# One gather per block of the second layer instead of three at once, and the next expert's first weight splits two blocks later

## The chip, the core and the metric

The program runs on one core of one Trainium2 chip. The metric is the time of one execution on the device in microseconds (us). The core's engines are called by their short names: PE multiplies matrices (PEld is its loading of weights), DVE works element by element, ACT evaluates functions, POOL is the general engine that here makes some element-wise work and issues all indirect DMAs, SP issues the plain DMAs. Each engine executes its own instructions strictly in program order and waits on semaphores for the others.

## The reference, cut to what matters

A gated linear attention over 4 x 768 tokens gives rows of 384 numbers. Each of the 3072 rows is then assigned to one of 8 experts (384 rows each, taken by the size of the router's logits), goes through that expert's two-layer network, and then through a second network that is the same for all rows:

```python
for e in range(E):                       # E = 8
    mask = assigned == e                 # 384 rows
    h = np.maximum(x[mask] @ w1[e], 0.0) # 384 -> 1024
    out[mask] = h @ w2[e]                # 1024 -> 384
...
h = x @ w_in                             # 384 -> 2048
sp = np.where(h > 20.0, h, np.log1p(np.exp(np.minimum(h, 20.0))))
g = h * np.tanh(sp)
return (g @ w_out).astype(np.float32)    # 2048 -> 384
```

All of it is float32. A product of float32 numbers is made of three matrix products: each operand is split into a rounded high part and a low remainder (`...h` and `...l` in the names), and high x high, low x high and high x low are added up.

## The kernel before, in words

The first 183 us are the attention and the routing of the first expert. Then a loop over the experts k = 0 to 7 runs (`for k in range(E)` in `tile_moe`), each with two phases on 384 gathered rows:

- the **first layer**, 8 blocks f of 128 hidden units: `h1` multiplies, `h1_parts` splits the result, `y1` multiplies by the second weight. The weight splits `split_w1(k, f)` (high part `w1h` on ACT, L914; low part `w1l` on POOL, L915) are made two blocks ahead, in two buffers each. Those of blocks 0 and 1 of the next expert are made during the second layer of this one.
- the **second layer**, 16 blocks f of 128 hidden units (`for f in range(GB)`). In a block PE makes `h2` (L945, L947: nine products, into one of the PSUM banks `h`) and then `o2` of an earlier block (L1064 and L1065 with the high part `gh`, then three products L1069 with the low part `gl`). From block 9 on that is `o2(f - 3)`.

Between them lies the activation, `mish(k, j)`, spread over ACT, DVE and POOL and over three calls: exp of block j (L1040, ACT) and its minimum with a constant (L1043, DVE, a `tensor_scalar`); square, log and exp of block j - 1 (L1022, L1026, L1029, ACT) and two combinations (L1034, L1047, DVE); the product of block j - 2 (L995, DVE), its high part `gh` (L1005, ACT) and its low part `gl` (L1014, POOL). So `gl` of block i is made after the exp of block i + 2, and PE asks for it in block i + 3. L1022 of the next call waits for L1043 of this one.

The rows of the next expert come through three indirect DMAs, one per 128 rows: `take_x(k, i)`, L907, issued by POOL into the tile `xg`. `gather(f)` at the end of each second-layer block runs whatever stands in the list `todo` and is ready: the loads of the next expert's weights once its number is known, then the three `take_x` once the indices `idx` (written on DVE, L886) are. For k = 1 to 5 the indices are there in block 9, so that all three gathers stand on POOL behind `gl(7)`; for k = 0 in block 7, behind `gl(5)`; for k = 6 before the second layer begins.

`trans_x(nxt, d)` transposes the gathered rows on PE in blocks 12, 13 and 14 (L935, three transpositions each, one per gathered part, all into the same PSUM bank `misc`), and the next call of `mish` splits what they leave (`split_p`: `xh` on ACT, L940, `xl` on DVE, L941). The transpositions of block 13 wait until `xl` of block 12 has emptied the bank. In block 12 the i-th transposition waits for the i-th gather alone.

During these blocks the routing of the expert after the next is computed too, in small DVE steps between the others (`step(...)`). For k = 0 the splits of the second network's weights (`w64.fine`) run beside it, with DVE, ACT and POOL work in nearly every block. In k = 6 no routing is left to do.

Of the kernel before, what the change touches and what calls it, by code (L numbers as in the profile page):

```python
# [653 lines left out]
def tile_moe(ctx, tc, L, x_d, w1_d, w2_d, winh, winl, wouth, woutl, ident, const, w64, choices, out):  # L654
# [3 lines left out]
    E, _, FF = w1_d.shape  # L658
# [251 lines left out]
    def split_w1(k, f):  # L910
        s = W[k][0][:, :, f * 128:(f + 1) * 128]
        ah = work.tile([128, KB, 128], F32R, name="w1h")
        al = work.tile([128, KB, 128], F32R, name="w1l")
        nc.scalar.activation(ah, s, AF.Copy)  # L914
        nc.gpsimd.tensor_sub(al, s, ah.bitcast(F32))  # L915
        W[k, f, 1] = (ah, al)

    def split_w2(k, f):
        s = W[k][1][:, f, :]
        bh = work.tile([128, DM], F32R, name="w2h", bufs=3)  # L920
        bl = work.tile([128, DM], F32R, name="w2l", bufs=3)
        nc.scalar.activation(bh, s, AF.Copy)
        nc.vector.tensor_sub(bl, s, bh.bitcast(F32))
        W[k, f, 2] = (bh, bl)
# [13 lines left out]
    def split_p(hl, d, p):  # L938
        h, l = hl
        nc.scalar.activation(h[:, d, :], p, AF.Copy)  # L940
        nc.vector.tensor_sub(l[:, d, :], p, h[:, d, :].bitcast(F32))  # L941
# [10 lines left out]
    def h1(k, f, ds):  # L952
        ah, al = W[k, f, 1]
        if ds[0] == 0:
            H1[k, f] = hbank()
        for d in ds:
            mm3(H1[k, f], ah[:, d, :], al[:, d, :], X[k][0][:, d, :], X[k][1][:, d, :], d == 0, d == KB - 1, k == f == 0)

    def h1_parts(k, f):
        p = H1[k, f]  # L960
        hh = work.tile([128, CAP], F32R, name="h1h", bufs=3)
        hl = work.tile([128, CAP], F32R, name="h1l", bufs=3)
        nc.scalar.activation(hh, p, AF.Relu)  # L963
        nc.vector.scalar_tensor_tensor(hl, p, 0.0, hh.bitcast(F32), op0=OP.max, op1=OP.subtract)
        H1[k, f] = (hh, hl)

    def y1(k, f, d):
        if (k, 0) not in A:
            A[k, 0] = acc_banks()
        bh, bl = W[k, f, 2]  # L970
        s = slice(d * 128, (d + 1) * 128)
        mm3(A[k, 0][d], bh[:, s], bl[:, s], H1[k, f][0], H1[k, f][1], f == 0, f == FB - 1)
# [82 lines left out]
    def o2(k, f, part=None, ts=None):  # L1055

        if (k, 1) not in A:
            A[k, 1] = acc_banks()
        gh, gl = G[k, f]
        ts = range(TB) if ts is None else ts  # L1060
        for t in ts:
            s = slice(t * 128, (t + 1) * 128)
            if part != 1:
                nc.tensor.matmul(A[k, 1][t], gh[:, s], wouth[:, f, :], start=f == 0, stop=False)  # L1064
                nc.tensor.matmul(A[k, 1][t], gh[:, s], woutl[:, f, :], start=False, stop=False)  # L1065
        for t in ts:
            s = slice(t * 128, (t + 1) * 128)
            if part != 0:
                nc.tensor.matmul(A[k, 1][t], gl[:, s], wouth[:, f, :], start=False, stop=f == GB - 1)  # L1069
# [3 lines left out]
    def finish(k, ts):  # L1073

        if ts[0] == 0:
            A[k, 2] = work.tile([128, TB, DM], F32, name="xg", bufs=1)
        for t in ts:
            if t == 1:
                nc.vector.tensor_scalar(A[k, 2][:, t, :], A[k, 1][t], 2.0, None, op0=OP.mult)
            else:  # L1080
                nc.scalar.activation(A[k, 2][:, t, :], A[k, 1][t], AF.Copy, scale=2.0)

    def put(k, t):

        i = nc.gpsimd.indirect_dma_start(
            out=out, out_offset=bass.IndirectOffsetOnAxis(ap=R[k]["idx"][:, t:t + 1], axis=0),
            in_=A[k, 2][:, t, :], in_offset=None)
        for other in SCAT:
            tc.declare_no_dep(i.ins, other.ins, reason="tokens of different slots are different rows")
        SCAT.append(i)  # L1090
# [30 lines left out]
    def step(part):  # L1121
        if due[0] == part:
            due[0] = next(rt, None)
# [18 lines left out]
    for k in range(E):  # L1142
        nxt = k + 1
        todo = [(take_w1, 0), (take_w2, 0)] + [(take_x, i) for i in range(TB)]

        def gather(f):
            if nxt == E:
                return
            while todo and (todo[0][0] is take_x and "idx" in R[nxt]
                            or todo[0][0] is not take_x and nxt in R and "e" in R[nxt]):  # L1150
                fn, i = todo.pop(0)
                fn(nxt, i)

        for f in range(FB):
            def convert():

                if k == 0 and f:
                    w64.fine(1)

            go = f >= 2 or k == 0  # L1160
            if k and f < LC:
                o2(k - 1, GB - LC + f)
            h1(k, f, [0])
            if k:
                mish(k - 1, GB + f)
            if go:
                step("fold")
            h1(k, f, [1])
            if go:
                step("ok")  # L1170
                convert()
                step("late")
            h1(k, f, [2])
            if go:
                step("cmp")
                step("take")
            convert()
            if k and f == LC - 1:
                finish(k - 1, range(TB))
            if f:  # L1180
                split_w2(k, f - 1)
            if f >= LB:
                y1(k, f - LB, 0)
            convert()
            for d in range(1, KB):
                if go and d == 1 + (f == FB - 1):
                    step("count")
                if f >= LB:
                    y1(k, f - LB, d)
            if go:  # L1190
                step("ct")
            h1_parts(k, f)
            if f + 2 < FB:
                split_w1(k, f + 2)
            if k and 0 <= f - 3 < TB:
                put(k - 1, f - 3)
        split_w2(k, FB - 1)
        Y[k] = (work.tile([128, KB, CAP], F32R, name="yh", bufs=1),
                work.tile([128, KB, CAP], F32R, name="yl", bufs=1))
        for d in range(KB):  # L1200
            for f in range(FB - LB, FB):
                y1(k, f, d)
                if d == 0 and f == FB - LB:
                    step("fold")
                    step("ok")
                if d == 1 and f == FB - LB:
                    step("late")
                    step("cmp")
                if d == KB - 1 and f == FB - 1:
                    step("count")  # L1210
            split_p(Y[k], d, A[k, 0][d])
        xnext = None
        if k == 0:
            assert w64.done()
            w64.on(work, ((("xh", "xl"), 1), ("h1h", 3), ("h1l", 3)))
            w64.part(32)
        for f in range(GB):
            if k == 0:
                w64.fine(1)
            go = f >= 4  # L1220
            assert k or w64.n["parts"] > 2 * f and w64.n["parts"] > min(31, 2 * f - 5), (f, w64.n)
            h2(k, f, [0])
            if f == 3 or go:
                step("fold")
            h2(k, f, [1, 2])
            x = None

            def middle():
                if f == 0 or go:
                    step("cmp")  # L1230
                    step("take")

            def after_g():
                if go:
                    step("ok")
                    step("late")

            x, xnext = xnext, None
            mish(k, f, after_g, middle, x)

            ready = [f - LC - 1] if LC < f <= 8 else []
            if f >= 8:
                ready.append(f - LC)
            for i in ready[:1]:
                o2(k, i, 0)
            if f == 0 or go:
                step("count")
            for i in ready[:1]:
                o2(k, i, 1)
            for i in ready[1:]:  # L1250
                o2(k, i)
            if go:
                step("ct")
            if nxt < E and 12 <= f < 12 + KB:
                xnext = trans_x(nxt, f - 12)
            if f >= 13:
                step("begin")
            gather(f)
            if nxt < E and 10 <= f < 12:
                split_w1(nxt, f - 10)  # L1260
        while todo and nxt < E:
            fn, i = todo.pop(0)
            fn(nxt, i)
# [70 lines left out]
```

## Time and profile before

| | us |
|---|---|
| three runs | 886.01, 889.72, 889.76 |
| median | 889.72 |
| the profiled execution | 887.8 |
| its span, first to last instruction | 885.8 |
| PE busy | 821.1 |
| DVE busy | 691.9 |
| ACT busy | 540.5 |
| POOL busy | 398.6 |

The profiled execution lies inside the spread of the three runs, 1.9 us under their median. The span is what the rows' times count from (0 is the first instruction), and 2.0 us of the profiled execution lie outside it. The busy times are sums over the whole program; an engine that is busy may still be waited for in one stretch and idle in the next, so the rows further down look at single stretches.

### The profile page before, as it was taken

Reading aid. Unit: us, or ns where it says so; the run is one execution under the profiler, and the core shown is the slowest. Engines: PE = TensorE matmul, PEld = TensorE weight load, DVE = VectorE, ACT = ScalarE, POOL = GpSimd, SP = SyncE. Lnnn points to the kernel's source line nnn. Section 1 sums busy time; section 2 is a strip of 40 time slices with the busy share of each in tenths; the row PEclk is TensorE's granted clock in tenths of the full one; section 3 lists DMA queues with packets and bytes.
Section 4 is the critical chain, followed back from the end, with each engine's and each line's share of the span. In section 5 each row is a group of like instructions: output and inputs, shape, how many; then the busy total and the mean of one; then the engine's idle time right before and its main releaser. Section 6 shows DMA issues by size and latency. Waiting matters only on the chain.

```text
span 885.8 us, 16971 instructions
## 1 busy us (share of the span) xinstructions
PE 821.1 (93%) x6162; PEld 765.1 (86%) x6162; DVE 691.9 (78%) x1734; ACT 540.5 (61%) x1283; POOL 398.6 (45%) x395
## 2 busy tenths in 40 slices
PE   7999999467998999999989999999999999999996
PEld 6888888356888999899989998899889889999995
DVE  5678998779899769877986798779878885765564
ACT  5666676214577547745864676376737663884684
POOL 4667887134146414541545154316432543545143
PEclk8999999759999999999999999999999999999999
DMA  9999994252410003002100310030004104100000
GB/s 169 198 235 221 219 219 123 93 189 86 180 47 17 10 29 135 27 19 78 75 28 23 135 36 5 28 143 28 0 28 143 27 1 168 30 1 21 8 1 27
DMA packets 127862, 71.97 MB, mean 81 GB/s; under 512 B 102944, under 2 KB 120352, under 8 KB 127776
## 3 DMA queue, kind: packets, MB, share of 16 engines
q1 hardware_dynamic: 124576, 61.41, 26.2%
q0 software_dynamic: 3072, 9.44, 3.3%
q8 instruction: 50, 0.82, 0.4%
q14 instruction: 36, 0.29, 0.1%
q10 hardware_dynamic: 128, 0.01, 0.0%
HBM read 61.35 MB, written 9.44 MB: 80 GB/s over the span
## 4 chain that ended last, share of the span: by engine, by line
PE 42%; DVE 15%; issue 9%; ACT 8%; POOL 6%; DMA 1%; SPq 0%; POOLq 0%; DVEq 0%; ACTq 0%
PE h L947 13%; PE acc L947 7%; PE h L945 7%; POOL gl L1014 4%; PE acc L945 4%; PE acc L1069 3%; PE acc L1064 3%; PE acc L1065 3%; DVE e L1034 2%; DVE e L1043 2%; ACT e L1022 2%; ACT r L1026 2%; DVE e L1047 2%; ACT r L1029 2%; DVE g L995 2%
## 5 line engine op out<-in xcount | busy, mean ns | idle before, releaser
L1014 POOL TENSOR_TENSOR gl<-g,gh 128x384 fp32r<-128x384 f32 x127 | 160.5, 1264 | 297.9 <-ACT gh L1005 295.4
L945 PE MATMUL h<-yh,winh 128*128 128x384 f32 x384 | 132.5, 345 | 0.3 <-DVE g L995 0.2
L1064 PE MATMUL acc<-wouth,gh 128*128 128x384 f32 x384 | 130.1, 339 | 1.2 <-ACT gh L1005 0.5
L947 PE MATMUL h<-yh,winl 128*128 128x384 f32 x384 | 129.5, 337 | 0.0
L947 PE MATMUL h<-yl,winh 128*128 128x384 f32 x384 | 129.4, 337 | 0.0
L1065 PE MATMUL acc<-woutl,gh 128*128 128x384 f32 x384 | 129.3, 337 | 0.0
L1034 DVE SCALAR_TENSOR_TENSOR e<-e,r 128x384 f32<-128x384 f32 (+2 forms) x154 | 74.7, 499 | 38.0 <-ACT r L1029 37.5
L1022 ACT ACTIVATE e<-e 128x384 f32<-128x384 f32 (+2 forms) x154 | 69.7, 469 | 50.5 <-DVE e L1043 48.0
L1069 PE MATMUL acc<-wouth,gl 128*128 128x384 f32 x384 | 90.5, 343 | 10.5 <-POOL gl L1014 9.9
L915 POOL TENSOR_TENSOR w1l<-w1r,w1h 128x384 fp32r<-128x384 f32 x64 | 66.5, 1039 | 70.9 <-ACT w1h L914 68.8
L963 ACT ACTIVATE h1h<-h 128x384 fp32r<-128x384 f32 x64 | 31.5, 492 | 109.4 <-PE h L947 109.2
L1043 DVE TENSOR_SCALAR e<-e 128x384 f32<-128x384 f32 (+2 forms) x154 | 83.4, 553 | 15.8 <-ACT e L1040 15.7
L1005 ACT ACTIVATE gh<-g 128x384 fp32r<-128x384 f32 (+2 forms) x154 | 68.9, 464 | 26.8 <-DVE g L995 26.4
L1069 PEld LDWEIGHTS acc<-wouth,gl 128*128 128x128 f32 x384 | 66.7, 188 | 17.8 <-POOL gl L1014 17.1
L1047 DVE SCALAR_TENSOR_TENSOR e<-e,r 128x384 f32<-128x384 f32 (+2 forms) x154 | 78.7, 524 | 0.2
L1064 PEld LDWEIGHTS acc<-wouth,gh 128*128 128x128 f32 x384 | 72.0, 187 | 4.6 <-ACT gh L1005 4.4
L995 DVE SCALAR_TENSOR_TENSOR g<-e,h 128x384 f32<-128x384 f32 (+2 forms) x154 | 71.7, 480 | 4.1
L945 PEld LDWEIGHTS h<-yh,winh 128*128 128x128 f32 x384 | 72.2, 188 | 1.6 <-issue 0.5
L947 PEld LDWEIGHTS h<-yl,winh 128*128 128x128 f32 x384 | 72.2, 188 | 0.8
L1040 ACT ACTIVATE e<-h 128x384 f32<-128x384 f32 (+2 forms) x154 | 62.6, 424 | 16.6 <-PE h L947 16.6
L1065 PEld LDWEIGHTS acc<-woutl,gh 128*128 128x128 f32 x384 | 72.1, 188 | 0.0
L947 PEld LDWEIGHTS h<-yh,winl 128*128 128x128 f32 x384 | 72.1, 188 | 0.0
(239 smaller groups left out, 2042.8 us busy)
## 6 DMA issues: line engine op xcount, KB each, us to landing
w1r<-in_moe_w_dram SPq DMA_DIRECT2D x8, 1536.0 KB, 6.6
w2r<-in_moe_w_dram SPq DMA_DIRECT2D x8, 1536.0 KB, 9.6
f<-in_f_logit_dram SPq DMA_DIRECT2D x24, 192.0 KB, 3.9
qq<-in_q_dram SPq DMA_DIRECT2D x24, 192.0 KB, 4.3
kk<-in_k_dram SPq DMA_DIRECT2D x24, 192.0 KB, 4.4
vp<-in_v_dram SPq DMA_DIRECT2D x24, 192.0 KB, 4.3
x_rows<-xs SPq DMA_DIRECT2D x24, 192.0 KB, 3.2
cv_raw<-in_moe_w_in_dram SPq DMA_DIRECT2D x9, 384.0 KB, 4.2
```

The costliest lines, as they stand in the source:

```text
L945: nc.tensor.matmul(p, wh, xh, start=start, stop=False)
L947: nc.tensor.matmul(p, w, x, start=False, stop=stop and w is (wh if late_x else wl))
L995: nc.vector.scalar_tensor_tensor(g[:, c], s2[:, c], 0.5, p[:, c], op0=OP.add, op1=OP.mult)
L1005: nc.scalar.activation(gh[:, c], g[:, c], AF.Copy)
L1014: nc.gpsimd.tensor_sub(gl, g, gh.bitcast(F32))
L1022: nc.scalar.activation(s[:, c], s[:, c], AF.Square, bias=1.0)
L1034: nc.vector.scalar_tensor_tensor(s[:, c], s[:, c], 1.0, r[:, c], op0=OP.add, op1=OP.mult)
L1043: nc.vector.tensor_scalar(e[:, c], e[:, c], EXP20, None, op0=OP.min)
L1047: nc.vector.scalar_tensor_tensor(s[:, c], s[:, c], 2.0, r[:, c], op0=OP.subtract, op1=OP.mult)
L1064: nc.tensor.matmul(A[k, 1][t], gh[:, s], wouth[:, f, :], start=f == 0, stop=False)
L1065: nc.tensor.matmul(A[k, 1][t], gh[:, s], woutl[:, f, :], start=False, stop=False)
L1069: nc.tensor.matmul(A[k, 1][t], gl[:, s], wouth[:, f, :], start=False, stop=f == GB - 1)
```

## The change

`gather` now stops after one `take_x`, so each call issues one gather; the three stand in blocks 9, 10 and 11 for k = 1 to 5 and in blocks 7, 8 and 9 for k = 0. The two first weight splits of the next expert move from blocks 10 and 11 to blocks 12 and 13.

```diff
                             or todo[0][0] is not take_x and nxt in R and "e" in R[nxt]):
                 fn, i = todo.pop(0)
                 fn(nxt, i)
+                if fn is take_x:
+
+                    break
 
         for f in range(FB):
@@ -1256,8 +1259,8 @@
             if f >= 13:
                 step("begin")
             gather(f)
-            if nxt < E and 10 <= f < 12:
-                split_w1(nxt, f - 10)
+            if nxt < E and 12 <= f < 14:
+                split_w1(nxt, f - 12)
```

POOL's order in the second layer of experts 1 to 5, from `gl(7)` (the last of the eight in the first row) to `gl(11)` and beyond. Before:

```order
L1014 TENSOR_TENSOR gl<-g,gh 128x384 x8
L907 DMA xg<-x_rows,idx 128x384 x3
L1014 TENSOR_TENSOR gl<-g,gh 128x384
L915 TENSOR_TENSOR w1l<-w1r,w1h 128x384
L1014 TENSOR_TENSOR gl<-g,gh 128x384
L915 TENSOR_TENSOR w1l<-w1r,w1h 128x384
L1014 TENSOR_TENSOR gl<-g,gh 128x384 x5
```

And now:

```order
L1014 TENSOR_TENSOR gl<-g,gh 128x384 x8
L907 DMA xg<-x_rows,idx 128x384
L1014 TENSOR_TENSOR gl<-g,gh 128x384
L907 DMA xg<-x_rows,idx 128x384
L1014 TENSOR_TENSOR gl<-g,gh 128x384
L907 DMA xg<-x_rows,idx 128x384
L1014 TENSOR_TENSOR gl<-g,gh 128x384
L915 TENSOR_TENSOR w1l<-w1r,w1h 128x384
L1014 TENSOR_TENSOR gl<-g,gh 128x384
L915 TENSOR_TENSOR w1l<-w1r,w1h 128x384
L1014 TENSOR_TENSOR gl<-g,gh 128x384 x3
```

The second gather now stands behind `gl(8)` and the third behind `gl(9)`; the two `w1l` moved from behind `gl(8)` and `gl(9)` to behind `gl(10)` and `gl(11)`.

ACT's order of the same experts in block 13 and the end of block 12, with the change (names: `e` and `r` are the activation's tiles, `xh<-misc` the high part of the transposed rows):

```order
L914 ACTIVATE w1h<-w1r 128x384
L1022 ACTIVATE e<-e 128x384
L1026 ACTIVATE r<-e 128x384
L1029 ACTIVATE r<-r 128x384
L940 ACTIVATE xh<-misc 128x384
L1040 ACTIVATE e<-h 128x384
L1005 ACTIVATE gh<-g 128x384
L914 ACTIVATE w1h<-w1r 128x384
```

The `w1h` in the first and the last of these rows stood in blocks 10 and 11 before; now they stand on either side of the block that also splits the first transposed rows.

## Rows read from the trace of the kernel before

**Rows 1.** The page: busy time, share of the span and instructions of each engine.

```profile
PE 821.1 (93%) x6162; PEld 765.1 (86%) x6162; DVE 691.9 (78%) x1734; ACT 540.5 (61%) x1283; POOL 398.6 (45%) x395
```

**Rows 2.** Stretches from block 11 to the next first layer, k = 1, 3, 5, 6.

```profile
core 0: us, PE busy (x) PEld busy (x) DVE busy (x) ACT busy (x) POOL busy (x), PEclk, DMA share, GB/s
356.80:378.62 21.82, 19.65 (x110) 17.96 (x110) 19.59 (x40) 15.47 (x34) 11.40 (x11) 1.00 0.10 28
...
527.12:549.16 22.04, 19.58 (x109) 17.86 (x109) 19.80 (x41) 15.72 (x35) 11.67 (x11) 1.00 0.10 28
...
698.34:720.13 21.79, 19.60 (x109) 17.86 (x109) 19.44 (x34) 15.49 (x34) 11.42 (x11) 1.00 0.10 28
779.69:797.98 18.29, 18.29 (x109) 18.15 (x109) 12.35 (x25) 15.65 (x33) 9.04 (x8) 1.00 0.00 1
```

**Rows 3.** Timeline of PE, k = 3: start, us, line, idle before and its releaser.

```profile
531.37 0.79 PE L1069 MATMUL acc<-wouth,gl 128*128 128x384 f32 x3 [1.45 <-POOL gl L1014]
...
535.16 0.49 PE L935 MATMUL misc<-ident,xg 128*128 128x128 f32 x3
...
539.77 0.55 PE L935 MATMUL misc<-ident,xg 128*128 128x128 f32 x3 [0.60 <-DVE xl L941]
...
543.29 0.49 PE L935 MATMUL misc<-ident,xg 128*128 128x128 f32 x3
```

**Rows 4.** Timeline of POOL, k = 3, from `gl(7)` on.

```profile
524.99 1.45 POOL L1014 TENSOR_TENSOR gl<-g,gh 128x384 fp32r<-128x384 f32 x1 [2.14 <-ACT gh L1005]
526.58 0.99 POOL L907 DMA_INDIRECT xg<-x_rows,idx  x1
527.88 1.16 POOL L907 DMA_INDIRECT xg<-x_rows,idx  x1 [0.31 <-issue]
529.35 0.95 POOL L907 DMA_INDIRECT xg<-x_rows,idx  x1 [0.30 <-issue]
530.31 1.00 POOL L1014 TENSOR_TENSOR gl<-g,gh 128x384 fp32r<-128x384 f32 x1
...
533.21 1.01 POOL L915 TENSOR_TENSOR w1l<-w1r,w1h 128x384 fp32r<-128x384 f32 x1
```

**Rows 5.** Timeline of DVE, k = 3: the minimum L1043 of blocks 10 and 11.

```profile
527.28 0.47 DVE L1043 TENSOR_SCALAR e<-e 128x384 f32<-128x384 f32 x1
...
530.01 4.42 DVE L1043 TENSOR_SCALAR e<-e 128x384 f32<-128x384 f32 x1
```

**Rows 6.** Timeline of ACT, k = 3.

```profile
527.04 0.52 ACT L1005 ACTIVATE gh<-g 128x384 fp32r<-128x384 f32 x1
527.46 0.52 ACT L914 ACTIVATE w1h<-w1r 128x384 fp32r<-128x384 f32 x1
...
529.78 0.52 ACT L1005 ACTIVATE gh<-g 128x384 fp32r<-128x384 f32 x1
...
534.47 0.53 ACT L1022 ACTIVATE e<-e 128x384 f32<-128x384 f32 x1 [3.77 <-DVE e L1043]
```

**Rows 7.** The tile xg, 515 to 540 us (k = 3): its three gathers, issue to landing.

```profile
DMA to landing us min/median/max: 3.1/3.2/3.3
```

**Rows 8.** Stretches, columns as in rows 2: k = 3 tails, then a block and tails of k = 6.

```profile
535.16:549.16 14.00, 12.99 (x73) 11.62 (x72) 12.65 (x34) 11.54 (x25) 5.21 (x4) 1.00 0.00 1
543.29:549.16 5.87, 5.57 (x31) 4.94 (x31) 5.83 (x18) 4.33 (x9) 2.05 (x2) 1.00 0.00 0
...
782.84:785.99 3.15, 3.15 (x19) 3.12 (x19) 2.11 (x4) 2.77 (x6) 2.22 (x3) 1.00 0.00 0
785.99:797.98 11.99, 11.99 (x73) 11.88 (x72) 8.12 (x17) 10.10 (x22) 4.61 (x4) 1.00 0.01 1
792.93:797.98 5.05, 5.05 (x31) 5.01 (x30) 3.30 (x7) 4.37 (x10) 2.10 (x2) 1.00 0.00 0
```

**Rows 9.** Timeline of PE, k = 0.

```profile
267.35 0.79 PE L1069 MATMUL acc<-wouth,gl 128*128 128x384 f32 x3 [1.59 <-POOL gl L1014]
...
282.36 0.55 PE L935 MATMUL misc<-ident,xg 128*128 128x128 f32 x3 [1.26 <-DVE xl L941]
...
286.86 0.55 PE L935 MATMUL misc<-ident,xg 128*128 128x128 f32 x3 [0.81 <-DVE xl L941]
```

## The prediction

> **What bounds the kernel now.** I read the page first: PE is busy 93% of the span [rows 1], so the kernel can gain only where PE stands still, and other engines matter through the waits that they cause. So the next view is the stretches of one expert after another, cut at PE's own instructions: from the first product of second-layer block 11 to the next first layer. In k = 6 this takes 18.29 us and PE is busy for all of it; in k = 1 to 5 it takes 21.79 to 22.04, and PE is busy for 19.6 [rows 2]. The products are the same; k = 6 differs in that its gathers came long before and that no routing is left. So up to 3.5 to 3.75 us per expert are to be had, five times.
>
> The timelines of k = 3 show where they go. PE waits 1.45 us for the low part `gl(8)` [rows 3]. On POOL `gl(8)` stands behind three gathers: it starts at 530.31, though its high part was there at 527.04 + 0.52 = 527.56 [rows 4, 6]. The second loss is less plain. L1043, the minimum on DVE, takes 0.47 us in block 10 and 4.42 in block 11 [rows 5]. The long one starts at 530.01, during the third gather, and ends at 534.43; POOL works without a gap from that gather through `gl(8)`, `w1l`, `gl(9)`, `w1l` until 534.22 [rows 4]. The short one starts during the first gather, which ends at 527.57 with a gap of 0.31 behind it, and ends 0.18 us after that. I read this as DVE's minimum getting no access while POOL issues without a gap. ACT then waits 3.77 us for it [rows 6], the activation runs late, and the transposition of block 13 waits for `xl` [rows 3]. From the first transposition to the next first layer k = 3 needs 14.00 us and k = 6 needs 11.99 [rows 8]. Of these 2.01 us, 5.87 - 5.05 = 0.82 lie behind the last transposition [rows 8], where the routing steps fill DVE (5.83 of 5.87 us); I leave those in place. The other 1.19 I put down to the late DVE.
>
> **The change, part by part (k = 3 stands for k = 1 to 5).**
>
> *The gather wait goes.* `gl(8)` now stands behind one gather. It starts when its high part is there, at 527.6, and takes 1.0 to 1.45 us (the two lengths of `gl` in rows 4): it ends by 529.05. PE could start the low products of block 11 at 531.37 - 1.45 = 529.92 [rows 3]: no wait, 1.45 us gained, and the first transposition is due at 535.16 - 1.45 = 533.71.
>
> *A new wait comes.* The third gather was issued at 529.35 and landed 3.1 to 3.3 us after its issue [rows 4, 7], before 532.7, long before the transposition at 535.16. Now it stands behind `gl(9)`. Worked along POOL: second gather at 528.75 to 529.2 (0.15 us behind `gl(8)`, as 526.58 stands behind 526.44 in rows 4), length 0.99 to 1.16, end 529.75 to 530.35; `gl(9)` when its high part is there (529.78 + 0.52 = 530.3 [rows 6]), 1.0 to 1.45 long, end 531.25 to 531.8; third gather at 531.4 to 531.95; landing, by 3.2, at 534.6 to 535.15. I take the middle, 534.9. The third transposition of block 12 would be due some 0.24 us after the first, at 533.95, so PE waits 0.95 us (0.65 to 1.2). Behind PE stands all of block 13. So of the 1.45 us two thirds are handed back.
>
> *The late DVE goes.* In blocks 10 and 11 POOL now has a gap before or behind every gather, and no string of four. L1043 of block 11 comes at about 529.9, during the second gather; even if `gl(9)` follows without a gap, it is held until 531.5 at most, not 534.4. PE is itself held up at the transpositions until 534.9, so ACT and DVE catch up. From there the stretch should go as in k = 6: 11.99 - 0.24 = 11.75 us, plus the 0.82 of routing, so the first layer starts at 534.9 + 11.75 + 0.82 = 547.47 instead of 549.16. **1.7 us per expert**, 1.4 to 2.0 by the two ends of the landing; 2.5 if the 0.82 goes as well. k = 1 and 5 start from 21.82 and 21.79 instead of 22.04 [rows 2], with `gl(8)` ready some 0.2 us earlier after the block's start; I take the same 1.7. Five experts: 8.5 us.
>
> *The splits move.* ACT gets two `w1h` of 0.52 us [rows 6] fewer in blocks 10 and 11 and as many more in 12 and 13. In k = 6 the three blocks from the first transposition hold 10.10 us of ACT work in 11.99, and a block with a `w1h` holds 2.77 in 3.15 [rows 8]; both have 0.38 us or more per block free, and what is short is covered by PE's new wait. `w1l` makes strings of two on POOL (`gl(10)`, `w1l`), at most 1.45 + 1.01 us; k = 6 has such strings before, without a wait on PE. The splits are used in the next first layer, over 8 us later. I cost this at nothing. If that cover is missing, it is up to 0.5 us per expert.
>
> *k = 0.* There PE waits 1.59 us for `gl(6)` behind the gathers, and 1.26 and 0.81 us at the transpositions of blocks 13 and 14 [rows 9]. The gathers now end in block 9, three blocks before the transpositions, so no new wait; the 1.59 go. But the weight splits of the second network run beside, and now `gl`, `w1l` and a `w64` part stand in one string in blocks 12 and 13, some 3.0 to 3.5 us in blocks of 3.15, so DVE may lose there what it won. Bounds 0 and 3.0, taken 1.5. *k = 6* has its gathers before the layer: 0.
>
> **Sum:** 8.5 + 1.5 = 10.0 us. The profiled execution took 887.8, so it would take 877.8; it stood 1.9 under the median of the runs (889.72), on which the same sum gives **879.7**. Its own range: 5 x 1.4 + 0.6 = 7.6 to 5 x 1.9 + 3.0 = 12.5, so 877.2 to 882.1.
>
> The trace shows L1043 held through a whole string of POOL instructions, over four that started after it [rows 4, 5]. The Trainium skill, SBUF — State Buffer, "Who interferes with whom", says of a 2-port DVE operation and a GpSimd instruction that whoever issues first has the shared port pair for that one instruction and the other blocks until it ends. By that L1043 would have been done just after 530.30, when the gather ended; the row's 4.42 us speak against it, and the measurement decides. By the rule the forecast's sum would stay (the landing of the third gather sets it), but the next rival and the last would lose their cause.
>
> **The rivals.**
>
> *DVE locked out again.* L1043 of block 10 starts at 527.28 during the first gather, and got through in the gap of 0.31 behind it. Now `gl(8)` is ready at 527.6, 0.05 us after that gather ends. If that is too little, L1043 waits until 528.6 + 0.2 = 528.8 instead of 527.75; ACT, `gh(9)` and `gl(9)` move back by 1.05, the third gather is issued at about 532.7 and lands at 535.9, the first layer starts at 548.5: 0.7 us per expert, with 0.8 for k = 0 4.3 in all, **885.4**. For it: the long L1043 also started during a gather with `gl` close behind. Against: there `gl` had long been ready.
>
> *Exchange.* The 14.00 us tail is the routing's doing, not the late minimum's (DVE is busy for 12.65 of it). Then the first layer starts at 534.9 - 0.24 + 14.00 = 548.66: 0.5 per expert, with 0.5 for k = 0 3 us, **886.7**. Against: the wait for `xl` lies in block 13, where the routing has hardly begun.
>
> *Slower: the third gather comes too late.* The forecast breaks even when the third gather lands at 549.16 - 12.57 = 536.59 (12.57 being 11.75 + 0.82), that is, when it is issued after 533.4. If L1043 is held in block 10, its delay of 1.05 leaves the issue at 532.7, still before that; if it is held in block 11 too, behind `gl(9)`, and then behind `gl` and `w1l` in blocks 12 and 13, the tail stays at 14.00 or grows: 535.9 - 0.24 + 14.0 + 0.6 = 550.3, 1.1 us lost per expert, and 1.5 for k = 0 by its longer strings: 7 us, **896.7**.
>
> **How the numbers follow.** Forecast 0.52; locked out 0.20; exchange 0.18; slower 0.10. About 0.5%, or 4.4 us, is what a measurement of this kernel can tell from no change; the three runs alone lie 3.75 us apart. Faster by more: nearly all of the forecast and half of the locked-out case, 0.60. Slower by more: 0.09. The same: 0.31. The range goes from 877.0 (the forecast's lower end) over both middle cases with a little above the second, 889.0.
>
> **What would show it.** PE's wait for `gl(8)` gone in k = 1 to 5 and for `gl(6)` in k = 0; in block 12 PE waiting about 1 us for the DMA of `xg`; no L1043 above 1.6 us; no wait for `xl` in block 13; the stretches of rows 2 at about 20.3 us. It is wrong if the wait for `xg` is over 2 us, if an L1043 of 2 us or more stands in blocks 12 to 14, or if the stretches stay above 21.

## The result, and the profile after

| | before | after |
|---|---|---|
| median of 7 runs each, on one chip | 887.66 | 880.76 |
| lowest and highest | 884.78, 889.84 | 878.72, 884.77 |
| ratio, 95% interval | | 0.9919 [0.9894, 0.9944] |
| span of the profiled execution | 885.8 | 882.8 |

The change makes the kernel 6.9 us faster; 10.0 were forecast. The time itself, 880.76, lies only 1.1 above the predicted 879.7, and that nearness is partly luck: the gain fell 3.1 short, but the median of all seven runs of the kernel before is 2.1 us under that of the three that the forecast starts from.

The page of the kernel after: busy times, the chain that ended last, and three groups of instructions (busy us, mean ns of one, then idle time before it and its releaser).

```profile
PE 821.2 (93%) x6162; PEld 766.9 (87%) x6162; DVE 680.2 (77%) x1734; ACT 541.8 (61%) x1283; POOL 401.8 (46%) x395
...
PE 51%; issue 9%; POOL 9%; DVE 5%; DMA 3%; ACT 2%; POOLq 0%; SPq 0%; DVEq 0%; ACTq 0%
...
L1069 PE MATMUL acc<-wouth,gl 128*128 128x384 f32 x384 | 89.5, 341 | 1.8 <-POOL gl L1014 1.7
L1022 ACT ACTIVATE e<-e 128x384 f32<-128x384 f32 (+2 forms) x154 | 69.5, 468 | 29.9 <-DVE e L1043 27.8
...
L1043 DVE TENSOR_SCALAR e<-e 128x384 f32<-128x384 f32 (+2 forms) x154 | 58.5, 391 | 21.3 <-ACT e L1040 21.1
```

The same rows of the kernel before:

```profile
PE 42%; DVE 15%; issue 9%; ACT 8%; POOL 6%; DMA 1%; SPq 0%; POOLq 0%; DVEq 0%; ACTq 0%
...
L1069 PE MATMUL acc<-wouth,gl 128*128 128x384 f32 x384 | 90.5, 343 | 10.5 <-POOL gl L1014 9.9
L1022 ACT ACTIVATE e<-e 128x384 f32<-128x384 f32 (+2 forms) x154 | 69.7, 469 | 50.5 <-DVE e L1043 48.0
L1043 DVE TENSOR_SCALAR e<-e 128x384 f32<-128x384 f32 (+2 forms) x154 | 83.4, 553 | 15.8 <-ACT e L1040 15.7
```

PE is as busy as before [rows 1]. What went is waiting: 8.2 us of PE's waits for `gl`, and 25 us of DVE time in the minimum L1043, whose instructions are the same; ACT's waits for that minimum (L1022) fall from 48.0 to 27.8. Not all of it is gone from DVE: its busy time falls by 11.7 us only, as other instructions grew, the combinations L1034 and L1047 by 3.5 us each in the two pages. DVE and ACT fall from 23% to 7% of the chain. What came is more DMA in the chain, 3% after 1%. The waits of PE in the kernel after show it (us in total, times, longest):

```profile
PE misc L935 <- DMA xg<-x_rows,idx: 6.1, 5, 1.4
...
PE misc L935 <- DVE xl L941: 2.4, 2, 1.7
PE acc L1069 <- POOL gl L1014: 1.7, 9, 0.2
```

Five waits for the gather, one in each of experts 1 to 5, where the kernel before had none; the waits for `xl` fall from 5.1 us (7 times) to two, both in k = 0. The stretches of [rows 2], in the same columns, k = 3, 5 and 6 (block 11 to the next first layer):

```profile
527.39:548.10 20.71, 19.15 (x109) 17.98 (x109) 17.81 (x41) 16.13 (x35) 12.18 (x11) 1.00 0.11 30
696.80:717.15 20.35, 19.15 (x109) 17.99 (x109) 17.30 (x35) 15.95 (x34) 11.78 (x11) 1.00 0.11 30
776.70:794.99 18.29, 18.29 (x109) 18.14 (x109) 12.20 (x25) 15.63 (x34) 9.06 (x8) 1.00 0.00 1
```

For k = 1 to 5 the stretches, read from PE's timeline in both profiles, were 21.82, 22.04, 22.04, 22.02, 21.79 and are 20.67, 20.58, 20.71, 20.79, 20.35: 1.15 to 1.46 us less each, 6.6 together. In k = 0, blocks 9 to 15 fall from 29.74 to 28.95: 0.8. The sum, 7.4, is close to the 6.9 of the medians. The two profiled spans differ by 3.0 only, since in the profile after, taken of the slowest run (884.77), the first expert starts 2.8 us later, and 1.5 more lie in the part of k = 0 ahead of block 9: code that the change doesn't touch, and times that differ as much between profiles of one kernel (two profiles of the changed kernel have the first expert at 198.35 and 196.13). One more such difference hides among the experts: block 8 lasts 4.71 or 5.5 us, before and after, now in one expert and now in another; where PE waits for `gl(8)`, a long block 8 makes block 11 some 0.25 us shorter (4.62 against 4.88 before). So the stretches from block 11 on are compared here, not whole experts.

PE in k = 3 of the kernel after, for [rows 3] (start, us, idle before and its releaser):

```profile
533.71 0.38 PE L935 MATMUL misc<-ident,xg 128*128 128x128 f32 x2
535.38 0.33 PE L935 MATMUL misc<-ident,xg 128*128 128x128 f32 x1 [1.30 <-DMA xg<-x_rows,idx]
...
538.69 0.49 PE L935 MATMUL misc<-ident,xg 128*128 128x128 f32 x3
...
542.21 0.55 PE L935 MATMUL misc<-ident,xg 128*128 128x128 f32 x3
```

In block 12 two parts are transposed at once, then PE stands 1.30 us for the third gather (1.25, 1.19, 1.30, 1.38 and 0.95 in k = 1 to 5). Blocks 13 and 14 follow without a wait. POOL in the same stretch, for [rows 4]:

```profile
526.87 0.98 POOL L907 DMA_INDIRECT xg<-x_rows,idx  x1 [0.15 <-issue]
527.92 1.02 POOL L1014 TENSOR_TENSOR gl<-g,gh 128x384 fp32r<-128x384 f32 x1
529.09 1.12 POOL L907 DMA_INDIRECT xg<-x_rows,idx  x1
530.65 1.45 POOL L1014 TENSOR_TENSOR gl<-g,gh 128x384 fp32r<-128x384 f32 x1 [0.45 <-ACT gh L1005]
532.24 0.97 POOL L907 DMA_INDIRECT xg<-x_rows,idx  x1
```

And DVE, for [rows 5]:

```profile
527.55 0.47 DVE L1043 TENSOR_SCALAR e<-e 128x384 f32<-128x384 f32 x1
527.94 1.41 DVE L1047 SCALAR_TENSOR_TENSOR e<-e,r 128x384 f32<-128x384 f32 x1
...
530.39 0.35 DVE L1043 TENSOR_SCALAR e<-e 128x384 f32<-128x384 f32 x1
```

The minimum of block 11 takes 0.35 us where it took 4.42. What is held now is the combination L1047 right behind the minimum of block 10, for 1.41 us (0.55 otherwise): it starts 0.02 us after `gl(8)` and ends 0.41 after it. That costs nothing here: `gh(9)` stands behind the exp of block 11 on ACT and comes 2.65 us after the block's start, as in the kernel before (529.78 - 527.12 [rows 6, 2]).

### The profile page after: what moved, and what is told of

It reads as the page before. It is cut to its first block, busy times and chain, and to the rows that moved or that the text cites. A ratio compares the mean times of both kernels' runs of the same rounds, so it can differ in the third digit from the quotient of the medians.

```text
span 882.8 us, 16971 instructions
## 1 busy us (share of the span) xinstructions
PE 821.2 (93%) x6162; PEld 766.9 (87%) x6162; DVE 680.2 (77%) x1734; ACT 541.8 (61%) x1283; POOL 401.8 (46%) x395
## 4 chain that ended last, share of the span: by engine, by line
PE 51%; issue 9%; POOL 9%; DVE 5%; DMA 3%; ACT 2%; POOLq 0%; SPq 0%; DVEq 0%; ACTq 0%
PE h L947 17%; PE h L945 9%; PE acc L947 8%; POOL gl L1014 6%; PE acc L1069 4%; PE acc L945 4%; PE acc L1064 4%; PE acc L1065 4%; DMA xg<-x_rows,idx 2%; POOL xg L907 1%; POOL w1l L915 1%; DVE cmp L696 1%; PE misc L773 1%; DMA w1r<-in_moe_w_dram 1%; ACT gh L1005 1%
## 5 line engine op out<-in xcount | busy, mean ns | idle before, releaser
L1014 POOL TENSOR_TENSOR gl<-g,gh 128x384 fp32r<-128x384 f32 x127 | 162.8, 1282 | 288.9 <-ACT gh L1005 284.3
L1034 DVE SCALAR_TENSOR_TENSOR e<-e,r 128x384 f32<-128x384 f32 (+2 forms) x154 | 78.2, 522 | 34.7 <-ACT r L1029 34.2
L1022 ACT ACTIVATE e<-e 128x384 f32<-128x384 f32 (+2 forms) x154 | 69.5, 468 | 29.9 <-DVE e L1043 27.8
L1005 ACT ACTIVATE gh<-g 128x384 fp32r<-128x384 f32 (+2 forms) x154 | 69.0, 464 | 28.4 <-DVE g L995 27.8
L1047 DVE SCALAR_TENSOR_TENSOR e<-e,r 128x384 f32<-128x384 f32 (+2 forms) x154 | 82.2, 548 | 0.2
L995 DVE SCALAR_TENSOR_TENSOR g<-e,h 128x384 f32<-128x384 f32 (+2 forms) x154 | 71.8, 480 | 4.1
L1043 DVE TENSOR_SCALAR e<-e 128x384 f32<-128x384 f32 (+2 forms) x154 | 58.5, 391 | 21.3 <-ACT e L1040 21.1
```

The costliest lines, as they stand in the source:

```text
L995: nc.vector.scalar_tensor_tensor(g[:, c], s2[:, c], 0.5, p[:, c], op0=OP.add, op1=OP.mult)
L1005: nc.scalar.activation(gh[:, c], g[:, c], AF.Copy)
L1014: nc.gpsimd.tensor_sub(gl, g, gh.bitcast(F32))
L1022: nc.scalar.activation(s[:, c], s[:, c], AF.Square, bias=1.0)
L1034: nc.vector.scalar_tensor_tensor(s[:, c], s[:, c], 1.0, r[:, c], op0=OP.add, op1=OP.mult)
L1047: nc.vector.scalar_tensor_tensor(s[:, c], s[:, c], 2.0, r[:, c], op0=OP.subtract, op1=OP.mult)
```

## The experiments

The theory: the gathers, one per block, take away both the queue ahead of `gl(8)` and the string of POOL work that held DVE; PE's new wait for the third gather hands part back, and the splits' place does nothing by itself. The first rival: the splits' move breaks up the string and earns the gain. The second: what holds DVE is peculiar to the minimum L1043. A table of all runs first; the third and fourth columns are, from each profile, the sum of the five stretches from block 11 to the next first layer (k = 1 to 5), and blocks 9 to 15 of k = 0.

| kernel | median us | k = 1 to 5 | k = 0 | ratio to before, interval |
|---|---|---|---|---|
| before (first profile) | 887.66 to 888.82 | 109.7 | 29.7 | |
| after | 880.76 | 103.1 | 29.0 | 0.9919 [0.9894, 0.9944] |
| after, once more | 880.76 | 103.7 | 29.0 | 0.9909 [0.9889, 0.9929] |
| gathers alone | 880.47 | 101.4 | 29.9 | 0.991 [0.9894, 0.9927] |
| splits alone | 885.35 | 106.0 | 28.5 | 0.9961 [0.9942, 0.9979] |
| minimum with an accumulator | 886.35 | 107.3 | 29.3 | 0.997 [0.9952, 0.9987] |
| two gathers, then one | 875.93 | 97.6 | 28.4 | 0.9852 [0.9835, 0.9868] |
| one gather, then two | 876.04 | 96.0 | 28.6 | 0.9843 [0.9818, 0.9868] |
| two, one; splits in 11, 12 | 878.89 | 101.3 | 29.1 | 0.9886 [0.9865, 0.9907] |
| two, one; splits in 10, 11 | 882.97 | 104.4 | 28.7 | 0.9924 [0.9906, 0.9943] |

### The two halves of the change

The kernel after with the splits put back:

```diff
-            if nxt < E and 12 <= f < 14:
-                split_w1(nxt, f - 12)
+            if nxt < E and 10 <= f < 12:
+                split_w1(nxt, f - 10)
```

> One gather per block, but the first weight splits stay in blocks 10 and 11. Theory (what counts is that gl(8) and the minimum L1043 no longer stand behind three gathers and a string of four): PE's wait for gl(8) is gone, the two w1l lengthen POOL's strings in blocks 10 and 11, so L1043 of block 11 is held 1 to 2 us, the third gather is issued no earlier than in the changed kernel, PE waits 1.3 to 1.8 us for it in block 12. From one first layer to the next in k = 3: 83.9 to 84.5 us (85.26 before, 83.94 changed); in all 4 to 6 us under before. Rival (the move of the splits does the work): the period stays at 85.0 to 85.3 and the time within 1.5 us of before.

Measured 880.47, the same as the whole change within the intervals, and 8.3 under the kernel before beside it, more than the 4 to 6 expected. The first rival, that the splits' move earns the gain, falls. PE waits 1.30 to 2.05 us for the third gather, somewhat longer than with the splits moved; a `w1l` now stands ahead of it on POOL. The minimum of block 11 is not held for 1 to 2 us as expected; the combination L1034 in front of it is, over the rest of the second gather, `w1l` and `gl(9)`, for 2.71 to 2.72 us in each of experts 1 to 5 (k = 3):

```profile
526.87 2.71 DVE L1034 SCALAR_TENSOR_TENSOR e<-e,r 128x384 f32<-128x384 f32 x1
```

PE stands at the third gather behind this, and no wait for `xl` follows in these experts. Block 15 takes 4.78 to 5.05 us instead of 5.6. So by the table the five experts are 1.7 us shorter in all than with the splits moved, and k = 0 loses 0.9, all that it had gained. Together that moves nothing that the intervals show.

The kernel before with only the splits moved:

```diff
-            if nxt < E and 10 <= f < 12:
-                split_w1(nxt, f - 10)
+            if nxt < E and 12 <= f < 14:
+                split_w1(nxt, f - 12)
```

> All three gathers at once as before, only the splits moved to blocks 12 and 13. Theory (L1043 is held for as long as POOL works without a gap): the string is now the third gather, gl(8), gl(9), so the long L1043 shrinks from 4.42 to about 2.4 us; PE's wait for gl(8) stays at 1.2 to 1.5 us, the wait for xl in block 13 goes, no wait for the gathers; period of k = 3 84.0 to 84.5 us, in all 3 to 6 us under before. Rival (the splits have nothing to do with it): L1043 still over 4 us, period 85.3, time as before.

The minimum of block 11 on DVE, PE's wait for `gl(8)` and its wait in block 14, k = 3:

```profile
529.60 2.58 DVE L1043 TENSOR_SCALAR e<-e 128x384 f32<-128x384 f32 x1
```

```profile
531.04 0.79 PE L1069 MATMUL acc<-wouth,gl 128*128 128x384 f32 x3 [1.45 <-POOL gl L1014]
...
542.19 0.55 PE L935 MATMUL misc<-ident,xg 128*128 128x128 f32 x3 [0.24 <-DVE xl L941]
```

The string behind the third gather is now `gl(8)` and `gl(9)` only, two instead of four, and the minimum is held 2.58 us instead of 4.42; the wait for `gl(8)` stays at 1.45 [rows 3], since the three gathers still stand ahead of it. The wait for `xl` in block 13 is gone, as expected; one of 0.24 to 0.30 us came in block 14. It earns 3.5 us. So the splits' move has a worth of its own, the late DVE, but the gathers' spreading takes the same loss away: the two halves don't add up (3.5 and 8.3 alone, each beside 888.82; 6.9 and 7.9 together in its two comparisons).

### Is it the minimum?

The kernel before, with the minima of blocks 9 to 11 written so that they also give an accumulated value that nobody uses:

```diff
             for c in cols(k, j):
-                nc.vector.tensor_scalar(e[:, c], e[:, c], EXP20, None, op0=OP.min)
+                if 9 <= j < 12:
+                    nc.vector.tensor_scalar(e[:, c], e[:, c], EXP20, None, op0=OP.min, op1=OP.max,
+                                            accum_out=small([128, 1], name="lim"))
+                else:
+                    nc.vector.tensor_scalar(e[:, c], e[:, c], EXP20, None, op0=OP.min)
```

> The kernel before, but L1043 of blocks 9 to 11 also writes out an accumulator (an unused maximum), nothing else changed. Theory (the plain form of the minimum needs something that POOL holds, and DVE's lateness costs the wait for xl): in this form it is not held, 0.4 to 0.8 us instead of 4.42; PE's wait for gl(8) stays at 1.45; the wait for xl of 0.60 goes; period of k = 3 about 84.1 us, in all about 5 us under before. Rival 1 (the tail is the routing's doing): L1043 short, but the wait for xl and the period of 85.3 stay. Rival 2 (any minimum on DVE is held): L1043 over 4 us, nothing changes.

DVE in k = 3 of that kernel (the lines behind L1043 stand four further down: L1044 is the minimum, L1051 the combination L1047):

```profile
532.04 0.55 DVE L1044 TENSOR_SCALAR_CACHE_REDUCE e<-e 128x384 f32<-128x384 f32 x1
...
532.51 4.25 DVE L1051 SCALAR_TENSOR_TENSOR e<-e,r 128x384 f32<-128x384 f32 x1
```

POOL beside it:

```profile
531.47 0.95 POOL L907 DMA_INDIRECT xg<-x_rows,idx  x1 [0.30 <-issue]
532.44 1.00 POOL L1014 TENSOR_TENSOR gl<-g,gh 128x384 fp32r<-128x384 f32 x1
533.39 1.01 POOL L915 TENSOR_TENSOR w1l<-w1r,w1h 128x384 fp32r<-128x384 f32 x1
534.37 1.00 POOL L1014 TENSOR_TENSOR gl<-g,gh 128x384 fp32r<-128x384 f32 x1
535.34 1.01 POOL L915 TENSOR_TENSOR w1l<-w1r,w1h 128x384 fp32r<-128x384 f32 x1
```

The single values of the theory came (0.4 to 0.8 us for the minimum, no wait for `xl`), the size of the gain did not: 2.5 us in all instead of 5, and 85.16 us for k = 3 (with a long block 8) instead of 84.1. The minimum goes through in 0.55 us beside a busy POOL, so the rival that any minimum is held falls; but the hold moves to the next instruction, which reads two tiles: 4.25 us, to 0.41 after the last `w1l`. So the hold is not peculiar to the minimum: DVE is late by the same string, at another instruction. The gain is what it brings that ACT no longer waits: L1022 needs the minimum, and only L995 needs the combination. The wait for `xl` is gone in experts 1 to 5, and in k = 3 the tail from the first transposition is 13.07 us instead of 14.00 [rows 8], though the routing is as before. Part of the gain is lost ahead of that: PE waits 1.57 to 1.94 us for `gl(8)`, where 1.45 was expected.

The Trainium skill, SBUF — State Buffer, "Who interferes with whom", lists this too: a DVE instruction with two SBUF inputs contends with a GpSimd instruction that reads SBUF, and among the operations that can take the shared port pair it counts `tensor_scalar`, but not the form that also writes out its accumulator. Both agree with these rows (4.25 and 0.55 us). That the loser is blocked only until the one instruction of the winner ends does not: L1047 stood 4.25 us beside four that follow one another.

### Without the new wait

If the wait for the third gather is what hands part of the gain back, the third must be issued one block earlier, with a string no longer than now. Two gathers in block 9 and one in block 10, the kernel after with:

```diff
-                if fn is take_x:
+                if fn is take_x and i:
```

> The changed kernel with two gathers in block 9 and the third in block 10, so that the third is issued one block earlier. Theory (the wait for the third gather is what the change gave back): gl(8) starts some 1 us later and PE waits 0 to 0.4 us for it; the third gather is issued at about 530.2 on the clock of k = 3, lands 0.5 us before PE needs it, the wait of 1.3 us in block 12 is gone; period of k = 1 to 5 about 82.7 to 83.2 us instead of 83.9, in all 4 to 6 us under the changed kernel (874 to 877). Rival (PE's wait only covered for late DVE and ACT work): the wait comes back at the transposition of block 13 for xl, and the time stays within 1.5 us of the changed kernel.

POOL in k = 3 of it, and PE (the products with `gl(8)` in block 11 and the transpositions of block 12):

```profile
523.45 0.99 POOL L907 DMA_INDIRECT xg<-x_rows,idx  x1
524.74 1.16 POOL L907 DMA_INDIRECT xg<-x_rows,idx  x1 [0.30 <-PE acc L1069]
525.93 1.03 POOL L1014 TENSOR_TENSOR gl<-g,gh 128x384 fp32r<-128x384 f32 x1
527.12 1.11 POOL L907 DMA_INDIRECT xg<-x_rows,idx  x1 [0.16 <-issue]
528.23 1.04 POOL L1014 TENSOR_TENSOR gl<-g,gh 128x384 fp32r<-128x384 f32 x1
```

```profile
527.01 0.79 PE L1069 MATMUL acc<-wouth,gl 128*128 128x384 f32 x3
...
530.79 0.49 PE L935 MATMUL misc<-ident,xg 128*128 128x128 f32 x3
```

875.93, in the expected 874 to 877: 4.8 us under the changed kernel, and the stretches fall to 19.45 to 19.71, 1.2 to 1.4 above those of k = 6. The third gather is issued 3.7 us before the transpositions of block 12 begin and needs 3.2, so nothing waits for it. `gl(8)` behind two gathers ends at 526.96, 0.05 us before PE's products with it; block 11 is 3.40 us long instead of 3.16. The rival, a wait for `xl` in its place, did not come: the two that are left are in k = 0, where the changed kernel has them too.

The other order, one gather and then two:

```diff
-                if fn is take_x:
+                if fn is take_x and i == 0:
```

> The changed kernel with one gather in block 9 and two in block 10. Theory (the third gather has to be issued one block earlier; gl(8) must not stand behind two gathers): no wait for gl(8), the third gather issued 1.3 us behind gl(8), landing 0.2 to 0.5 us before PE needs it, gl(9) behind it held back to within 0.2 us of PE; period of k = 1 to 5 82.7 to 83.4 us, in all 12 to 15 us under before, no worse than two in block 9. Rival (gl(9) now takes the place of gl(8)): PE waits 0.3 us or more for gl(9) in block 12, 1 to 3 us slower than two in block 9.

876.04, the same within the intervals. PE does not wait for `gl(9)`, so its rival did not come. Its stretches are shorter by 0.3 each, 0.5 once (block 11 is 3.15 us instead of 3.40), but in its profile block 8 had its long form in all five experts, in that of the other order in four. Which of the two is better stays open; both beat the kernel before and the change.

### The splits' place without that cover

With one gather per block the splits' place did not show in the time (880.76 and 880.47). There PE stood at the third gather anyway. Now the two kernels with the splits earlier, both with two gathers and one:

```diff
-            if nxt < E and 12 <= f < 14:
-                split_w1(nxt, f - 12)
+            if nxt < E and 10 <= f < 12:
+                split_w1(nxt, f - 10)
```

> Two gathers in block 9 and one in block 10, with the first weight splits back in blocks 10 and 11. Theory (a DVE instruction that reads two tiles, or the plain minimum, waits through the whole string of POOL instructions): the string is gl(8), gather, w1l, gl(9), w1l; a DVE instruction of 2.5 us or more stands in block 11 and the wait for xl in block 13 comes back with 0.3 to 0.7 us; period 83.2 to 84.0, 1 to 4 us slower than with the splits in blocks 12 and 13. Rival (only the place of the gathers matters, and block 15 is shorter without the splits in block 13, as it was in the run with the gathers alone, 5.05 against 5.59 us): 1 to 3 us faster than with the splits in 12 and 13.

DVE's combination L1034 in block 12, and PE's wait, k = 3:

```profile
532.69 3.21 DVE L1034 SCALAR_TENSOR_TENSOR e<-e,r 128x384 f32<-128x384 f32 x1 [0.59 <-ACT r L1029]
```

```profile
538.96 0.55 PE L935 MATMUL misc<-ident,xg 128*128 128x128 f32 x3 [1.09 <-DVE xl L941]
```

882.97, 7.0 us slower than with the splits in blocks 12 and 13, more than the 1 to 4 expected; the rival, that it is faster, falls. Behind the third gather (530.44 to 531.54) POOL runs `w1l`, `gl`, `w1l` and `gl` without a gap to 535.48; L1034 starts in it and ends at 535.90. The wait for `xl` of [rows 3] is back, 1.09 to 1.11 us in experts 1 to 5.

One block later, `11 <= f < 13` and `f - 11`:

> Two gathers in block 9 and one in block 10, the first weight splits in blocks 11 and 12. Theory: strings of two at most (gl(9), w1l and gl(10), w1l), nothing of the splits left in block 13, no DVE instruction over 1.5 us in blocks 10 to 13; block 15 shorter by up to 0.5 us as in the run with the gathers alone; 0 to 3 us faster than with the splits in blocks 12 and 13. Rival (block 15 hangs on the routing, not on the splits): same as with the splits in 12 and 13, within 1 us.

878.89, 3.0 us slower than with 12 and 13: a miss, since a gain was expected from a shorter block 15. Block 15 stays at 5.57, and PE waits 0.27 for `xl` in block 13. DVE there, and POOL beside it:

```profile
528.85 1.30 DVE L1034 SCALAR_TENSOR_TENSOR e<-e,r 128x384 f32<-128x384 f32 x1 [0.58 <-ACT r L1029]
530.07 1.16 DVE L1043 TENSOR_SCALAR e<-e 128x384 f32<-128x384 f32 x1
531.16 1.37 DVE L1047 SCALAR_TENSOR_TENSOR e<-e,r 128x384 f32<-128x384 f32 x1
```

```profile
527.73 1.03 POOL L1014 TENSOR_TENSOR gl<-g,gh 128x384 fp32r<-128x384 f32 x1
528.71 1.02 POOL L915 TENSOR_TENSOR w1l<-w1r,w1h 128x384 fp32r<-128x384 f32 x1
529.89 1.13 POOL L1014 TENSOR_TENSOR gl<-g,gh 128x384 fp32r<-128x384 f32 x1 [0.17 <-ACT gh L1005]
530.98 1.13 POOL L915 TENSOR_TENSOR w1l<-w1r,w1h 128x384 fp32r<-128x384 f32 x1
```

Three DVE instructions in a row each take 0.75 to 0.82 us longer than they do elsewhere (0.55 and 0.35). The rival, the same time within 1 us, fell as well.

Why block 15 is 5.6 us here and 5.05 or less with the gathers alone, the traces show in part. The last minimum ahead of block 15 and the `gl` beside it decide: where the minimum starts 0.1 to 0.2 us after that `gl`, it takes 0.98 to 1.12 us, and block 15 takes 5.56 to 5.63; where it is through before that `gl` starts, it takes 0.34 to 0.36, and block 15 takes 4.78 to 5.05. That holds in experts 0 to 6 of all ten profiles. First the kernel after, k = 3 (that `gl` starts at 541.85), then the gathers alone (538.98):

```profile
542.07 1.00 DVE L1043 TENSOR_SCALAR e<-e 128x384 f32<-128x384 f32 x1
```

```profile
538.52 0.36 DVE L1043 TENSOR_SCALAR e<-e 128x384 f32<-128x384 f32 x1
```

What lets DVE run ahead there was not tried.

The kernel after ran once more beside these:

> The changed kernel once more, on the chip of these runs, so that the others are compared with it directly: 0.990 to 0.994 of before; in block 12 of k = 1 to 5 a wait of 0.9 to 1.4 us for the third gather.

880.76 again (one of the five waits, 1.75 us, is longer than expected; the others are 1.19 to 1.25). The last four runs were made on another chip than the first four; the kernel before took 888.62 us there and 888.82 on the other, so the differences between these kernels are not the chip's.

## Why the prediction held, point by point

**The gather wait goes**: right. PE's 1.45 us for `gl(8)` is gone; the nine waits for a `gl` that are left have at most 0.2 us.

**A new wait comes**: right, and its size was short: 1.30 us in k = 3 where 0.95 was taken, 0.95 to 1.38 over the experts where 0.65 to 1.2 was allowed. The working put the third gather at 531.4 to 531.95; counted from the start of block 11 (0.27 us later in this profile, the difference between its count and the old one of the kernel before) it stands at 531.97. The upper end came because `gl(9)` took 1.45 us, the longer of the two lengths in [rows 4], with 0.14 us behind it. Landing, 3.14 us after the issue, was as read [rows 7]. So the landing came 0.21 us later than taken; and PE came to the third transposition 0.14 earlier, at 533.81 on the old count instead of 533.95. I took the middle of an interval with two discrete lengths; the row of the `gl` that starts after a wait of its own (`gl(7)`, 1.45) was the nearer one.

**The late DVE goes**: right in its core. No L1043 in blocks 10 and 11 is long; 1.01 us is the most in blocks 9 to 15 of k = 1 to 5, and no wait for `xl` is left there. Not foreseen: the combinations L1047 and L1034 are held as well. The tail from the landing was 12.72 us instead of 12.57. The 0.82 us behind the last transposition did stay, but the routing is not the reason for most of them: with the gathers alone and the same routing, these 5.87 us become 5.02 to 5.29, where the last minimum is not held beside `gl`.

So the first layer of k = 4 came at 548.10, 547.83 on the old count, instead of 547.47: 0.21 by the landing, 0.15 by the tail. **The term of 1.7 us per expert was the mis-sized one: the stretches show 1.33 for k = 3 and 6.6 for all five instead of 8.5.** The measured 6.9 lie below the 7.6 to 12.5 that the sum gave itself as a range (built with 0.6 and 1.9 where the parts say 0 and 2.0; with those it is 7.0 to 13.0).

**The splits cost nothing**: right in the time (880.76 against 880.47 with the splits left in place), but two effects hide in it: the move costs the five experts 1.7 us of their stretches, and earns k = 0 0.9. Without the cover of PE's new wait the prediction had the sign wrong. It feared up to 0.5 us per expert lost by moving the splits to blocks 12 and 13; there that place is the better one, by 3.0 and 7.0 us over the two earlier ones. What counts is not ACT's 0.52 us per split but `w1l` making POOL's strings longer, at which DVE is late.

**k = 0**: 0.8 where 1.5 was taken, inside its bounds. Block 9 gained 1.83 us by the wait for `gl(6)`, and more than half was given back behind it. One part was not foreseen: between blocks 10 and 11 a combination is held over the rest of the third gather, a part of the second network's split, and `gl`; block 12 is 4.16 us long where it was 3.40 (and is 3.38 with two gathers and one, where no instruction there is held longer than 1.05). DVE and POOL:

```profile
272.98 2.89 DVE L1034 SCALAR_TENSOR_TENSOR e<-e,r 128x384 f32<-128x384 f32 x1
```

```profile
272.32 1.11 POOL L907 DMA_INDIRECT xg<-x_rows,idx  x1
273.45 1.03 POOL L108 TENSOR_TENSOR woutl<-h1h,wouth 128x384 fp32r<-128x384 f32 x1
274.42 1.03 POOL L1014 TENSOR_TENSOR gl<-g,gh 128x384 fp32r<-128x384 f32 x1
```

The other part came as the prediction said it might, by the splits in blocks 12 and 13: the wait for `xl` in block 14 grew from 0.81 [rows 9] to 1.70. It is 1.72 with the splits alone and 0.82 with the gathers alone. **k = 6** changed by less than 0.01 us, as said.

**The rivals.** *Locked out again* did not come: L1043 of block 10 ended 0.10 us after `gl(8)` began, unheld (0.47 us); the instruction behind it was held instead, where it costs nothing. *Exchange* fell: counted as it counts (from 0.24 us ahead of the landing) the tail is 12.96 us and not 14.00, and the minimum with an accumulator shortened it with the routing and the gathers unchanged. *Slower* did not come: the third gather was issued at 531.97 on the old count, 1.4 us short of the 533.4 from which the change was to lose. No run issued it that late, so the threshold is not tested.

## What to carry to other kernels

A transfer's issue is an instruction in an engine's order: when it is moved behind a product, work out where it now stands in the queue and when it lands, because PE may wait for the landing instead of for the product. Here two gathers together, so that the third goes out a block earlier, gave 12.6 and 12.9 us against 6.9 and 7.9 of the even spread. And two cures for one loss don't add up: undo each by itself, and ask again what each is worth once the wait that covers it is gone.

## What the runs showed of the hardware that was not expected

How long a DVE instruction is held beside POOL depends, in these traces, on what heads POOL's string. Behind a gather, where POOL goes on within 0.04 us, it stood through everything that followed: 4.42 us beside four (before), 4.25 (the accumulator kernel), 3.21 (two gathers and one, splits early), 2.89 (k = 0 after), 2.71 (gathers alone), 2.58 (splits alone). In the ten profiles there are 60 cases of L1034, L1043 or L1047 that reach past the gather into such a string, and none ended before the string did: the minimum 0.22 to 0.23 us after its end, the combinations 0.41 to 0.43. Where no gather heads the string, as in the last pair of rows of the splits in 11 and 12, DVE got in between two POOL instructions, and both took somewhat longer (`gl` and `w1l` 1.13 instead of 1.00). It is not the length that decides: in k = 0 of the kernel after POOL runs six without a gap and no gather at their head, and L1034, L1043 and L1047 take 0.83, 0.69 and 1.37 us beside them. Also new was that the held instruction may be one that reads two tiles as well as the minimum, and that the form with an accumulator was not held at all (0.55 us); nor was the product L995, which reads one of its two inputs from PSUM (0.53 to 0.56 us beside `gl` and `w1l` in all profiles). Why a gather at the head makes the difference was not tried by itself and stays open.
